# Reordered front of an attention and feed-forward kernel: scores two tiles ahead, fixed VectorE and ScalarE order, two units begun early

## The chip, the cores and the metric

The kernel runs on one core of a Trainium2 chip. The metric is the time of one execution on the device in microseconds (us); the median of 3 runs of the kernel before is 967.41 us (967.27 to 970.9). Names of engines in the trace: PE is TensorE (PEld its weight loads), DVE is VectorE, ACT is ScalarE, POOL is GpSimd, SP is the queue that issues most DMAs.

## The reference: attention, then two feed-forward layers

```python
q_d, k_d, v_d = means of q, k, v over groups of factor=4 positions
out_up    = repeat(softmax(scale * q_d @ k_d.T) @ v_d, 4)     # 144 x 144 per head
scores    = where(abs(pos_i - pos_j) < 4, scale * q @ k.T, -1e9)
out_local = softmax(scores) @ v                               # a band of 7 keys per query
x   = (out_up + out_local) as 2304 tokens x 512
h   = silu(x @ w_gate) * (x @ w_val);  x2  = h @ w_out        # d_ff 1536
h2  = x2 @ w_in;  out = (h2 * clip(h2 + 3, 0, 6) / 6) @ w_out2  # d_ff 2048
```

Four batches, 8 heads, 576 positions, head size 64. The weights arrive as 64-bit numbers and are decoded to 32 bits on the chip.

## The kernel before: a front, then a stream of units

**Blocks and units.** The 2304 tokens are worked in five blocks of 512, 384, 512, 512 and 384 columns. For each block the feed-forward layers run as 68 units, each of 128 rows of a weight: G and V (gate and value), O (out), H and P (second layer). A unit of G, V or H is 12 matmuls into one of two PSUM banks named mm: x and the weights are each split into a high and a low part, and high x high, low x high and high x low are added for four chunks of 128 rows. Attention for batches 1 to 3 runs on VectorE beside the units.

**The front.** Batch 0's attention has no units to hide behind. It is done by `first_batch` on TensorE, 0 to about 64 us of the span. First q and k are turned (`load_T`), with the downsampled attention (`down_scores`, `down_trans`, `down_values`, four chunks of two heads) in between. Then the band is worked in five tiles of 122 queries, the last of 88. For a tile, `scores(i)` makes the masked scores on TensorE, takes the maxima on VectorE (fnm) and the exponentials with their sums on ScalarE (held, eight instructions); `norm(i)` divides on VectorE; `trans(i)` turns the weights on TensorE, ahead of which stand `fill` matmuls on constants (FILL_P of them), and copies the two halves back, one by ScalarE and one by VectorE (turned); `values(i)` multiplies with the values on TensorE, adds the downsampled part, and `put_cols` writes the tile's columns of x (xr), high part by ScalarE, low part by VectorE. PSUM banks are few: tile 0, 2, 4's scores share acc0 and acc1, tile 1, 3's share the mm banks, all turnings share acc2 and acc3, and `down_trans`, `down_values` and `values` share pa and px.

**Weights.** `prefetch(i)` issues five steps for units ahead: load (raw 64-bit, four buffers), `decode_a` on ScalarE (top), `decode_b` on VectorE (w), the copy to `kept`, and `split_unit` (wr, high part on ScalarE, low part on VectorE, for a pair of units). A raw buffer is free for the next load once `decode_b` has read it.

**What sets the order.** Each engine works through its own queue in the order that the program is built with. Instructions under `tc.keep_in_program_order` stand in the order of the code; the others are placed by the scheduler where it expects them to be ready. In the kernel before, the front's matmuls are pinned, VectorE's and ScalarE's work of the front is mostly not, and weight steps are pinned (`behind`) only until `first_batch` ends. `run_unit` splits unit 0 (HALVES = 1) into columns 0 to 244 and 244 to 512, unpinned, so the scheduler put four of its matmuls between those of the last tiles.

Of the kernel before, what the change touches and what calls it, by code (L numbers as in the profile page):

```python
# [32 lines left out]
HALVES = 1  # L33
# [10 lines left out]
FILL_P = (4, 8, 8, 8, 8)  # L44
# [3 lines left out]
def tile_kernel(  # L48
# [85 lines left out]
    front = [True]  # L134

# [134 lines left out]
    def put_cols(bi, col, xv):  # L270

        if bi not in xr:
            xr[bi] = sp.tile([P, NC, 2, UMAX * UT], F32R, tag="xr", name=f"xr{bi}")
        dst = xr[bi][:, :, :, col:col + xv.shape[2]]
        nc.scalar.activation(dst[:, :, 0], xv, AF.Copy)
        nc.vector.tensor_tensor(dst[:, :, 1], xv, dst[:, :, 0].bitcast(F32), op=ALU.subtract)
# [39 lines left out]


    def first_batch():
# [6 lines left out]
        with tc.tile_pool(name="fp", bufs=1) as fp:  # L325
# [125 lines left out]
            for base, sgn in ((-UPAD, -1), (UPAD + 3, 1)):  # L451
                nc.gpsimd.affine_select(
                    out=ups, in_=ups, compare_op=ALU.is_ge, fill=0.0,
                    base=base, pattern=[[-sgn, UPAD + 3 * QT]], channel_multiplier=4 * sgn,
                )
            kT = fp.tile([P, NC, S + 6], F32, name="fkT")
            nc.vector.memset(kT[:, :, :3], 0.0)
            nc.vector.memset(kT[:, :, S + 3:], 0.0)
# [12 lines left out]
            def load_T(w, c):  # L471
                src = qn[w, c // 2]
                for th in range(2):
                    tag = ("acc0", "acc1", "mm", "mm")[turn[0] % 4]
                    turn[0] += 1
                    ps = bank(tag, f"fT{w}{c}{th}", 2 if tag == "mm" else 1)
                    ps = ps[:, :3 * (TT + GJ)].rearrange("p (t n) -> p t n", t=3)
                    for t in range(3):
                        tc.keep_in_program_order(nc.tensor.matmul(
                            ps[:, t], src[:, 3 * th + t, c % 2 * 2:c % 2 * 2 + 2].rearrange("j h d -> j (h d)"),  # L480
                            turner, start=True, stop=True,
                        ))
                    dst = qT[:, c, th * S // 2:(th + 1) * S // 2] if w == "q" else \
                        kT[:, c, 3 + th * S // 2:3 + (th + 1) * S // 2]
                    dst = dst.rearrange("p (t j) -> p t j", t=3)
                    small = (ds if w == "q" else dk)[:, c, th * NJH:(th + 1) * NJH].rearrange("p (t j) -> p t j", t=3)
                    if w == "q":
                        nc.vector.tensor_scalar(dst, ps[:, :, :TT], 0.125, None, op0=ALU.mult)
                        nc.scalar.activation(small, ps[:, :, TT:], AF.Copy, scale=1 / 128)
                    else:  # L490
                        nc.scalar.activation(dst, ps[:, :, :TT], AF.Copy)
                        nc.vector.tensor_copy(small, ps[:, :, TT:])
# [7 lines left out]
            def down_scores(c):  # L500
# [14 lines left out]
                for par in range(2):  # L515
                    nc.vector.tensor_reduce(nm[:, par], pss[par], axis=AX.X, op=ALU.max, negate=True)
                    for half in range(2):
                        nc.scalar.activation(
                            pd[:, par, half], pss[par][:, half], AF.Exp, bias=nm[:, par, half:half + 1],
                        )  # L520
# [4 lines left out]
            def down_trans(c):  # L525
                pd = dst[c]
                for par in range(2):
                    h = 2 * c + par
                    pt = trans_d(lambda qh: pd[:, par, qh], bank(("pa", "px")[par], f"fdT{h}"), together)
                    dpt[h] = fp.tile([NJH, 2, NJ], F32, tag="fdpT", name=f"fdpT{h}", bufs=8)  # L530
                    nc.scalar.activation(dpt[h], pt, AF.Copy)

            def down_values(c):
# [9 lines left out]
                nc.vector.tensor_scalar(sd, po[:, :, :, D:], EPS, 4.0, op0=ALU.add, op1=ALU.mult)  # L543
                nc.vector.reciprocal(sd, sd)
                nc.vector.tensor_tensor(
# [8 lines left out]
            first_max = []  # L554

            def scores(i):
# [27 lines left out]
                for par in range(2):  # L584
                    ps = pss[par][:n, :, :w_]
                    nc.vector.tensor_reduce(nm[:n, :, par], ps, axis=AX.X, op=ALU.max, negate=True)
                    for c in range(NC):
                        nc.scalar.activation(
                            p_[:n, c, par, :w_], ps[:, c], AF.Exp, bias=nm[:n, c, par:par + 1],
                            accum_out=sm[:n, c, par:par + 1],  # L590
                        )
                pe[i], tot[i] = p_, sm
                if i == 0:
                    first_max.append(nm[:n, 0, :1])

            def norm(i):
                n = size(i)
                w_ = n + 6
                nc.vector.tensor_scalar(tot[i][:n], tot[i][:n], EPS, None, op0=ALU.add)
                nc.vector.reciprocal(tot[i][:n], tot[i][:n])  # L600
                nc.vector.tensor_tensor(
# [8 lines left out]
            def trans(i):  # L610
# [3 lines left out]
                for hh in range(2):  # L614
# [9 lines left out]
                    if hh:  # L624
                        nc.vector.tensor_copy(to, ps[:w_, :, :, :n])
                    else:
                        nc.scalar.activation(to, ps[:w_, :, :, :n], AF.Copy)
# [27 lines left out]
            for c in range(NC):  # L655
# [6 lines left out]
                if c == 2:  # L662
                    prefetch(3 - LR)
# [6 lines left out]
            next(ahead)  # L670
            down_values(0)
            down_values(1)
            norm(0)
            trans(0)
            prefetch(4 - LR)
            down_trans(3)
            down_values(2)
            norm(1)
            scores(2)
            down_values(3)  # L680
            prefetch(5 - LR)
            values(0)
            for i in range(1, NT):
                next(ahead, None)
                next(ahead, None)
                trans(i)
                if i + 2 < NT:
                    scores(i + 2)
                if i == 1:
                    prefetch(6 - LR)  # L690
                if i == 2:
                    prefetch(7 - LR)
                if i + 1 < NT:
                    norm(i + 1)
                next(ahead, None)
                values(i)
            for _ in ahead:
                pass
        front[0] = False
# [240 lines left out]
    HIGH, LOW = ((0, 0), (1, 0)), ((0, 1),)  # L940

    def run_unit(i):
# [3 lines left out]
        if kind in "GVH":  # L946
            ps = bank("mm", f"p{kind}{bi}_{f}", 2)[:, :nt]
            x = xr[bi] if kind != "H" else state["x2"]
            cols = [slice(0, nt)]
            if i < HALVES:  # L950
                cols = [slice(0, 244), slice(244, nt)]
            for cs in cols:
                for part in (HIGH, LOW):
                    for c in range(NC):
                        for a, b_ in part:
                            nc.tensor.matmul(  # L956
                                ps[:, cs], r[:, a, c], x[:, c, b_, cs],
                                start=part is HIGH and a == c == 0, stop=part is LOW and c == NC - 1,
                            )
# [93 lines left out]
    for bi in range(NB):  # L1053
# [34 lines left out]
        for i in range(bi * NU, (bi + 1) * NU):  # L1088
            m = i - bi * NU
            prefetch(i)  # L1090
# [66 lines left out]
```

## Time and profile before

| | us |
|---|---|
| median of 3 runs | 967.41 (967.27 to 970.9) |
| profiled execution | 967.38 |
| its span, first to last instruction | 965.7 |
| front: first instruction to the first matmul of unit 2 (pV) | 71.12 |
| mean granted TensorE clock | 0.993 |

A row of the timeline reads: start in us of the span, duration in us, engine, line, operation, output <- inputs, shape, how many in a row, and in brackets the idle time of that engine before it and what ended it. A duration contains the pipeline's latency, so the pace of an engine is taken from the starts of rows that follow each other.

### The profile page before, as it was taken

Reading aid. Unit: us, or ns where it says so; the run is one execution under the profiler, and the core shown is the slowest. Engines: PE = TensorE matmul, PEld = TensorE weight load, DVE = VectorE, ACT = ScalarE, POOL = GpSimd, SP = SyncE. Lnnn points to the kernel's source line nnn. Section 1 sums busy time; section 2 is a strip of 40 time slices with the busy share of each in tenths; the row PEclk is TensorE's granted clock in tenths of the full one; section 3 lists DMA queues with packets and bytes.
Section 4 is the critical chain, followed back from the end, with each engine's and each line's share of the span. In section 5 each row is a group of like instructions: output and inputs, shape, how many; then the busy total and the mean of one; then the engine's idle time right before and its main releaser. Section 6 shows DMA issues by size and latency. Waiting matters only on the chain.

```text
span 965.7 us, 13166 instructions
## 1 busy us (share of the span) xinstructions
PE 948.1 (98%) x4928; PEld 803.2 (83%) x4928; DVE 724.6 (75%) x1059; ACT 501.6 (52%) x928; POOL 110.4 (11%) x125
## 2 busy tenths in 40 slices
PE   9899999999999999999999999999999999999997
PEld 7687888777899988878888778888888788999996
DVE  4678976899979979999774799997337994445652
ACT  4666566876543567553333764443335445444542
POOL 7610002200062300014320000000000000000000
PEclk9999999999999999999999999999999999999999
DMA  8999799866799823359972222462322323443331
GB/s 195 228 270 340 247 366 311 183 198 236 261 246 264 166 86 109 99 188 242 199 157 88 88 67 67 173 216 90 97 100 93 103 88 108 154 131 130 120 122 33
DMA packets 116340, 160.80 MB, mean 167 GB/s; under 512 B 61868, under 2 KB 83756, under 8 KB 116276
## 3 DMA queue, kind: packets, MB, share of 16 engines
q1 hardware_dynamic: 67892, 131.41, 42.7%
q0 software_dynamic: 43488, 10.72, 11.1%
q10 hardware_dynamic: 4896, 17.83, 4.7%
q8 instruction: 39, 0.64, 0.3%
q14 instruction: 25, 0.20, 0.1%
HBM read 137.29 MB, written 22.54 MB: 166 GB/s over the span
## 4 chain that ended last, share of the span: by engine, by line
PE 78%; DVE 7%; DMA 1%; ACT 1%; issue 1%; ACTq 0%; DVEq 0%
PE pH L956 19%; PE aP L998 18%; PE aO L998 13%; PE pV L956 13%; PE pG L956 12%; DVE wr L239 2%; PE pS L881 1%; PE pO L731 1%; DMA w<-in_moe_w_out_dram 1%; DVE xf L856 1%; PE pPT L724 1%; PE px L847 1%; DMA w<-in_moe_w_gate_dram 1%; DVE pv L827 1%; DVE w L225 1%
## 5 line engine op out<-in xcount | busy, mean ns | idle before, releaser
L239 DVE TENSOR_TENSOR wr<-w,wr 128x1024 fp32r<-128x1024 f32 x170 | 207.8, 1222 | 123.8 <-ACT wr L238 123.6
L238 ACT ACTIVATE wr<-w 128x1024 fp32r<-128x1024 f32 x170 | 179.5, 1056 | 119.1 <-issue 57.7
L956 PE MATMUL pH<-x,wr 128*128 128x512 f32 (+1 forms) x960 | 212.2, 372 | 0.0
L998 PE MATMUL aP<-wr,gH 128*128 128x512 f32 x864 | 211.4, 395 | 0.3 <-ACT gH L973 0.3
L956 PEld LDWEIGHTS pH<-x,wr 128*128 128x128 f32 x960 | 173.1, 188 | 25.3 <-issue 2.9
L998 PEld LDWEIGHTS aP<-wr,gH 128*128 128x128 f32 x864 | 159.8, 188 | 34.8 <-issue 2.5
L956 PE MATMUL pG<-xr,wr 128*128 128x512 f32 (+3 forms) x732 | 156.4, 369 | 1.0 <-DVE sl L968 0.6
L956 PE MATMUL pV<-xr,wr 128*128 128x512 f32 (+1 forms) x720 | 153.9, 369 | 0.9 <-ACT sl L962 0.9
L998 PE MATMUL aO<-gV,wr 128*128 128x512 f32 (+1 forms) x720 | 154.4, 371 | 0.0
L956 PEld LDWEIGHTS pG<-xr,wr 128*128 128x128 f32 x732 | 133.3, 191 | 18.5 <-DVE sl L968 1.0
L998 PEld LDWEIGHTS aO<-gV,wr 128*128 128x128 f32 x720 | 132.4, 190 | 16.9 <-DVE gV L974 0.2
L956 PEld LDWEIGHTS pV<-xr,wr 128*128 128x128 f32 x720 | 130.8, 188 | 18.4 <-ACT sl L962 1.8
L971 ACT ACTIVATE h<-pH,consts 128x512 f32<-128x512 f32 (+1 forms) x80 | 51.4, 643 | 59.7 <-PE pH L956 59.5
L973 ACT ACTIVATE gV<-sl 128x512 fp32r<-128x512 f32 (+1 forms) x60 | 35.0, 584 | 85.5 <-DVE sl L968 85.2
L216 ACT ACTIVATE top<-w 128x512 f16<-128x512 bf16 x68 | 52.3, 790 | 22.9 <-DMA w<-in_moe_w_out_dram 7.7
L962 ACT ACTIVATE sl<-pG 128x512 f32<-128x512 f32 (+1 forms) x60 | 33.0, 551 | 59.6 <-PE pG L956 57.0
L973 ACT ACTIVATE gH<-h 128x512 fp32r<-128x512 f32 (+1 forms) x80 | 46.9, 586 | 31.9 <-DVE h L972 31.6
L972 DVE SCALAR_TENSOR_TENSOR h<-h,pH 128x512 f32<-128x512 f32 (+1 forms) x80 | 50.5, 632 | 15.6 <-ACT h L971 15.1
L790 DVE TENSOR_TENSOR pr<-q,k 128x1792 f32<-128x1792 f32 x27 | 54.6, 2021 | 9.4 <-DMA k<-in_k_dram 9.2
L974 DVE TENSOR_TENSOR gH<-h,gH 128x512 fp32r<-128x512 f32 (+1 forms) x80 | 50.6, 633 | 10.9 <-ACT gH L973 10.5
L827 DVE TENSOR_TENSOR pv<-sc,v 128x1792 f32<-128x1792 f32 x27 | 54.6, 2022 | 0.5
L793 DVE TENSOR_REDUCE sc<-pr 128x28 f32<-128x1792 f32 x27 | 54.4, 2015 | 0.1
(131 smaller groups left out, 761.9 us busy)
## 6 DMA issues: line engine op xcount, KB each, us to landing
w<-kept SPq DMA_DIRECT2D x136, 512.0 KB
kept<-w ACTq DMA_DIRECT2D x34, 512.0 KB
w<-in_moe_w_out_dram SPq DMA_DIRECT2D x28, 512.0 KB
w<-in_moe_w_in_dram SPq DMA_DIRECT2D x16, 512.0 KB
w<-in_moe_w_gate_dram SPq DMA_DIRECT2D x12, 512.0 KB
w<-in_moe_w_val_dram SPq DMA_DIRECT2D x12, 512.0 KB
out_dram<-os SPq DMA_DIRECT2D x16, 256.0 KB
dnq<-in_q_dram POOLq DMA_DIRECT2D x24, 144.0 KB, 7.8
```

What stands on the lines that cost most here:

```text
L216: behind(nc.scalar.activation(halves(top[i % 2], 2, F16)[:, :, 1], h3.bitcast(BF16), AF.Copy))
L238: behind(nc.scalar.activation(r[:, :, 0], s, AF.Copy))
L239: behind(nc.vector.tensor_tensor(r[:, :, 1], s, r[:, :, 0].bitcast(F32), op=ALU.subtract))
L790: nc.vector.tensor_tensor(pr, qt[:, a:a + SUB, None, :].to_broadcast([P, SUB, W, D]), win(kt, a, SUB), op=ALU.mult)
L793: nc.vector.tensor_reduce(sc[:, a:a + SUB], pr, axis=AX.X, op=ALU.add)
L827: nc.vector.tensor_tensor(pr, pe[:, a:a + SUB, :, None].to_broadcast([P, SUB, W, D]), win(vt, a, SUB), op=ALU.mult)
L956: nc.tensor.matmul(ps[:, cs], r[:, a, c], x[:, c, b_, cs], start=part is HIGH and a == c == 0, stop=part is LOW and c == NC - 1,)
L971: nc.scalar.activation(h, ps, AF.Relu, scale=1 / 6, bias=half1[:, 0:1])
L972: nc.vector.scalar_tensor_tensor(h, h, 1.0, ps, op0=ALU.min, op1=ALU.mult)
L973: nc.scalar.activation(g[:, 0, :nt], h, AF.Copy)
L974: nc.vector.tensor_tensor(g[:, 1, :nt], h, g[:, 0, :nt].bitcast(F32), op=ALU.subtract)
L998: nc.tensor.matmul(ps, **one, start=f_ == 0 and a == b_ == 0, stop=f_ == nf - 1 and b_ == 1,)
```

## The change

- In `first_batch`, `scores` is cut in two: matmuls and maxima stay, the exponentials become `weights(i)`, placed later in the code.
- In the loop over tiles the order is now `norm(i)`, `scores(i + 2)`, `values(i - 1)`, `trans(i)`, `weights(i + 2)`, then the weight prefetch; it was `trans(i)`, `scores(i + 2)`, prefetch, `norm(i + 1)`, `values(i)`.
- `vec` and `act` (class Ordered) pin every VectorE and ScalarE instruction of the front from `kT` on; `put_cols` is pinned by `behind`. The weight steps stay pinned until unit 3's prefetch (EARLY_W = 4).
- FILL_P goes from (4, 8, 8, 8, 8) to (4, 4, 4, 4, 0).
- HALVES = 2: `begin_unit`, pinned, works 244 columns of unit 0 after `values(2)` and 366 columns of unit 1 after `values(3)`; `run_unit` does columns 244 to 512 and 366 to 512 after the front.

```diff
-FILL_P = (4, 8, 8, 8, 8)
+EARLY_W = 4
+FILL_P = (4, 4, 4, 4, 0)
...
+    def begin_unit(i, n):
+        kind, f, bi = units[i]
+        ps = bank("mm", f"p{kind}{bi}_{f}", 2)
+        products(ps, split[i], xr[bi], slice(0, n), tc.keep_in_program_order)
+        begun[i] = ps, n
...
+            def weights(i):
+                n = size(i)
+                pss, nm = scored.pop(i)
+                for par in range(2):
+                    for c in range(NC):
+                        act.activation(
...
             scores(0)
             ahead = down_sums(1, ["qk"], first_max[0])
+            weights(0)
             down_trans(2)
             down_scores(3)
             scores(1)
+            weights(1)
...
             for i in range(1, NT):
                 next(ahead, None)
                 next(ahead, None)
-                trans(i)
+                norm(i)
                 if i + 2 < NT:
                     scores(i + 2)
                 if i == 1:
-                    prefetch(6 - LR)
+                    down_values(2)
+                    down_values(3)
+                values(i - 1)
+                if i >= NT - HALVES:
+                    begin_unit(i - NT + HALVES, (i - 1) * QT)
+                trans(i)
+                if i + 2 < NT:
+                    weights(i + 2)
+                    prefetch(4 + i - LR)
...
         for i in range(bi * NU, (bi + 1) * NU):
             m = i - bi * NU
+            front[0] = i < EARLY_W
             prefetch(i)
```

ScalarE after the last turning of k, before: fdT is chunk 2 of the downsampled weights turned, fdpT its copy, held tile 0's exponentials, fdpd chunk 3's.

```order
L491 ACTIVATE fkT<-fTk_439 128x288
L531 ACTIVATE fdpT_476<-fdT_471 72x288
L588 ACTIVATE held,fsm_445<-fS_0_447,fnm_446 122x128 x4
L588 ACTIVATE held,fsm_445<-fS_1_448,fnm_446 122x128 x4
L531 ACTIVATE fdpT_483<-fdT_478 72x288
L518 ACTIVATE fdpd_492<-fdS_485,fdnm_491 72x144 x2
```

In the changed kernel the same place of ScalarE's queue reads:

```order
L145 ACTIVATE fkT<-fTk_436 128x288
L145 ACTIVATE held,fsm_442<-fS_0_444,fnm_443 122x128 x4
L145 ACTIVATE held,fsm_442<-fS_1_445,fnm_443 122x128 x4
L145 ACTIVATE fdpT_473<-fdT_468 72x288
L145 ACTIVATE fdpT_480<-fdT_475 72x288
L145 ACTIVATE fdpd_489<-fdS_482,fdnm_488 72x144 x2
```

Both copies of chunk 2 now stand behind tile 0's eight exponentials, where the first stood ahead of them.

ScalarE around the split of units 0 and 1 (wr), before: held and fsm are tile 2's and then tile 3's exponentials and sums, xr and turned belong to tiles 0 and 1.

```order
L588 ACTIVATE held,fsm_612<-fS_0_614,fnm_613 122x128 x4
L588 ACTIVATE held,fsm_612<-fS_1_615,fnm_613 122x128 x4
L216 ACTIVATE top_159<-w_2_265 128x512
L238 ACTIVATE wr_655<-w_0_580 128x2x512
L275 ACTIVATE xr_671<-fO_658 128x4x122
L627 ACTIVATE turned<-fPT_0_678 128x488
L231 DMA kept_125<-w_0_580 128x1024
L588 ACTIVATE held,fsm_698<-fS_0_700,fnm_699 122x128 x4
```

In the changed kernel ScalarE's queue has there:

```order
L288 ACTIVATE xr_686<-fO_673 128x4x122
L145 ACTIVATE turned<-fPT_0_689 128x488
L145 ACTIVATE held,fsm_629<-fS_0_631,fnm_630 122x128 x4
L145 ACTIVATE held,fsm_629<-fS_1_632,fnm_630 122x128 x4
L229 ACTIVATE top_159<-w_2_265 128x512
L251 ACTIVATE wr_717<-w_0_620 128x2x512
```

VectorE in the same place, before (fsm and held in three rows are `norm(2)`):

```order
L225 SCALAR_TENSOR_TENSOR w_0_580<-w_1_257,top_161 128x512
L599 TENSOR_SCALAR fsm_612<-fsm_612 122x8
L600 RECIPROCAL fsm_612<-fsm_612 122x8
L601 TENSOR_TENSOR held<-held,fsm_612 122x1024
L239 TENSOR_TENSOR wr_655<-w_0_580,wr_655 128x2x512
L276 TENSOR_TENSOR xr_671<-fO_658,xr_671 128x4x122
L625 COPY turned<-fPT_1_692 128x488
```

In the changed kernel VectorE's queue has there:

```order
L289 TENSOR_TENSOR xr_686<-fO_673,xr_686 128x4x122
L145 COPY turned<-fPT_1_699 128x488
L238 SCALAR_TENSOR_TENSOR w_0_620<-w_1_257,top_161 128x512
L252 TENSOR_TENSOR wr_717<-w_0_620,wr_717 128x2x512
L145 TENSOR_SCALAR fsm_558<-fsm_558 122x8
L145 RECIPROCAL fsm_558<-fsm_558 122x8
L145 TENSOR_TENSOR held<-held,fsm_558 122x1024
```

The split of units 0 and 1 now stands behind tile 3's exponentials on ScalarE, and ahead of `norm(2)` on VectorE, where it stood behind `norm(2)` and ahead of tile 3's exponentials.

VectorE at the end of the front, before (w are decodings, wr_912 the split of units 2 and 3, wr_954 that of 4 and 5, the last xr rows tile 4's columns):

```order
L276 TENSOR_TENSOR xr_671<-fO_808,xr_671 128x4x122
L625 COPY turned<-fPT_1_841 128x488
L225 SCALAR_TENSOR_TENSOR w_4_910<-w_4_577,top_159 128x512
L239 TENSOR_TENSOR wr_912<-w_2_727,wr_912 128x2x512
L225 SCALAR_TENSOR_TENSOR w_4_910<-w_5_651,top_161 128x512
L276 TENSOR_TENSOR xr_671<-fO_850,xr_671 128x4x122
L625 COPY turned<-fPT_1_879 94x4x88
L225 SCALAR_TENSOR_TENSOR w_6_984<-w_6_724,top_159 128x512
L276 TENSOR_TENSOR xr_671<-fO_885,xr_671 128x4x24
L239 TENSOR_TENSOR wr_954<-w_4_910,wr_954 128x2x512
```

In the changed kernel the end of the front reads on VectorE:

```order
L289 TENSOR_TENSOR xr_686<-fO_851,xr_686 128x4x122
L145 COPY turned<-fPT_1_885 94x4x88
L289 TENSOR_TENSOR xr_686<-fO_891,xr_686 128x4x24
L289 TENSOR_TENSOR xr_906<-fO_891,xr_906 128x4x64
L238 SCALAR_TENSOR_TENSOR w_4_916<-w_4_617,top_159 128x512
L252 TENSOR_TENSOR wr_918<-w_2_789,wr_918 128x2x512
L238 SCALAR_TENSOR_TENSOR w_4_916<-w_5_713,top_161 128x512
L252 TENSOR_TENSOR wr_947<-w_4_916,wr_947 128x2x512
L238 SCALAR_TENSOR_TENSOR w_6_976<-w_6_786,top_159 128x512
```

Three decodings and the split of units 2 and 3 went from ahead of the last tile's columns to behind them.

## Rows read from the trace of the kernel before

**Rows 1.** The page, part 1: busy us (share of the span) and instructions.

```profile
PE 948.1 (98%) x4928; PEld 803.2 (83%) x4928; DVE 724.6 (75%) x1059; ACT 501.6 (52%) x928; POOL 110.4 (11%) x125
```

**Rows 2.** Timeline of PE in the front, 25 to 50 us.

```profile
25.16 1.25 PE L538 MATMUL fdO<-fvd,fdpT 72*72 72x65 f32 x16
...
26.63 1.25 PE L538 MATMUL fdO<-fvd,fdpT 72*72 72x65 f32 x16 [0.22 <-ACT fdpT L531]
...
30.08 0.75 PE L724 MATMUL fdT<-ident,fdpd 72*72 72x72 f32 x8 [0.92 <-DVE tmp L545]
...
33.03 1.57 PE L538 MATMUL fdO<-fvd,fdpT 72*72 72x65 f32 x16 [2.21 <-ACT fdpT L531]
...
41.37 1.05 PE L469 MATMUL fPT<-ident 128*128 128x256 bf16 x8
...
42.26 1.00 PE L620 MATMUL fPT<-ident,held 122*128 122x122 f32 x8
...
43.19 0.64 PE L572 MATMUL fS<-band,pick 64*122 64x512 bf16 x4
...
47.73 1.05 PE L469 MATMUL fPT<-ident 128*128 128x256 bf16 x8
```

**Rows 3.** Windows of 10 us: busy (instructions) by engine, granted clock, DMA share, GB/s.

```profile
30.00:40.00 10.00, 7.71 (x73) 6.39 (x74) 6.78 (x15) 5.12 (x25) 6.86 (x5) 0.83 1.36 226
60.00:70.00 10.00, 10.00 (x70) 8.81 (x69) 6.95 (x10) 6.28 (x10) 0.00 (x0) 0.83 0.92 320
340.00:350.00 10.00, 8.30 (x40) 7.87 (x39) 8.21 (x16) 4.14 (x8) 0.00 (x0) 0.83 0.32 106
```

**Rows 4.** Timeline of PE inside the third of those windows.

```profile
343.66 0.41 PE L847 MATMUL px<-ident,o 128*128 128x128 f32 x2 [1.70 <-DVE o L833]
```

**Rows 5.** Timeline of PE around units 0 to 2.

```profile
67.92 0.64 PE L956 MATMUL pG<-xr,wr 128*128 128x268 f32 x3
...
68.17 0.62 PE L956 MATMUL pG<-xr,wr 128*128 128x512 f32 x2
...
71.12 5.74 PE L956 MATMUL pV<-xr,wr 128*128 128x512 f32 x24
```

**Rows 6.** Timeline of ACT, 26 to 70 us.

```profile
26.16 0.42 ACT L531 ACTIVATE fdpT<-fdT 72x288 f32<-72x288 f32 x1
...
38.07 0.37 ACT L588 ACTIVATE held<-fS,fnm 122x128 f32<-122x128 f32 x1 [4.88 <-DVE fnm L586]
...
40.82 0.81 ACT L216 ACTIVATE top<-w 128x512 f16<-128x512 bf16 x1
...
42.39 0.61 ACT L275 ACTIVATE xr<-fO 128x488 fp32r<-128x488 f32 x1
...
64.23 0.25 ACT L275 ACTIVATE xr<-fO 128x96 fp32r<-128x96 f32 x1 [2.59 <-PE fO L644]
...
68.08 1.28 ACT L962 ACT_TABLE_LOAD   x1 [1.06 <-DVE w L225]
...
69.37 0.60 ACT L962 ACTIVATE sl<-pG 128x512 f32<-128x512 f32 x1
```

**Rows 7.** Timeline of DVE, 37 to 43 us.

```profile
37.34 1.29 DVE L586 TENSOR_REDUCE fnm<-fS 122x4 f32<-122x512 f32 x2 [1.88 <-PE fS L580]
...
38.55 0.15 DVE L543 TENSOR_SCALAR fdsd<-fdO 72x4 f32<-72x4 f32 x1
...
39.28 0.68 DVE L225 SCALAR_TENSOR_TENSOR w<-w,top 128x512 int32<-128x512 int32 x1
...
41.00 0.35 DVE L599 TENSOR_SCALAR fsm<-fsm 122x8 f32<-122x8 f32 x1 [1.04 <-ACT held L588]
...
42.76 1.22 DVE L239 TENSOR_TENSOR wr<-w,wr 128x1024 fp32r<-128x1024 f32 x1
```

**Rows 8.** Timeline of DVE and of PE in the first pass over units.

```profile
107.34 1.23 DVE L239 TENSOR_TENSOR wr<-w,wr 128x1024 fp32r<-128x1024 f32 x1
...
112.08 5.60 PE L956 MATMUL pG<-xr,wr 128*128 128x512 f32 x24
```

More of the change, by code (lines that the diff above doesn't have):

```diff
@@ L32 @@
 WARM = 14
-HALVES = 1
+HALVES = 2
 CLOAD = (0, 4)
@@ L134, in tile_kernel, with __init__, __getattr__, issue @@
     front = [True]
+    class Ordered:
+        def __init__(self, engine):
+            self.engine = engine
+        def __getattr__(self, name):
+            op = getattr(self.engine, name)
+            def issue(*args, **kw):
+                tc.keep_in_program_order(op(*args, **kw))
+            return issue
     def behind(ins):
@@ L315, in down_T, with products @@
             yield
+    HIGH, LOW = ((0, 0), (1, 0)), ((0, 1),)
+    begun = {}
+    def products(ps, r, x, cs, pin=lambda ins: None):
+        for part in (HIGH, LOW):
+            for c in range(NC):
+                for a, b_ in part:
+                    pin(nc.tensor.matmul(
+                        ps[:, cs], r[:, a, c], x[:, c, b_, cs],
+                        start=part is HIGH and a == c == 0, stop=part is LOW and c == NC - 1,
+                    ))
+    def begin_unit(i, n):
[3 more added lines that the diff above has]
+        begun[i] = ps, n
     def first_batch():
@@ L584, in scores @@
                 for par in range(2):
[L585 to L591, printed above, removed]
+                    vec.tensor_reduce(nm[:n, :, par], pss[par][:n, :, :w_], axis=AX.X, op=ALU.max, negate=True)
                 pe[i], tot[i] = p_, sm
+                scored[i] = pss, nm
                 if i == 0:
                     first_max.append(nm[:n, 0, :1])
+            def weights(i):
+                n = size(i)
+                pss, nm = scored.pop(i)
+                for par in range(2):
+                    for c in range(NC):
+                        act.activation(
+                            pe[i][:n, c, par, :n + 6], pss[par][:n, c, :n + 6], AF.Exp,
+                            bias=nm[:n, c, par:par + 1], accum_out=tot[i][:n, c, par:par + 1],
+                        )
             def norm(i):
@@ L668, in first_batch @@
             scores(1)
+            weights(1)
             next(ahead)
             next(ahead)
+            norm(0)
             down_values(0)
             down_values(1)
-            norm(0)
+            scores(2)
             trans(0)
+            down_trans(3)
+            prefetch(3 - LR)
+            weights(2)
             prefetch(4 - LR)
[L676 to L682, printed above, removed]
             for i in range(1, NT):
@@ L689, in first_batch @@
                 if i == 1:
-                    prefetch(6 - LR)
+                    down_values(2)
[7 more added lines that the diff above has]
+                    prefetch(4 + i - LR)
                 if i == 2:
                     prefetch(7 - LR)
-                if i + 1 < NT:
-                    norm(i + 1)
                 next(ahead, None)
-                values(i)
+            values(NT - 1)
             for _ in ahead:
                 pass
-        front[0] = False
         x_done[0] += NG
@@ L946, in run_unit @@
         if kind in "GVH":
-            ps = bank("mm", f"p{kind}{bi}_{f}", 2)[:, :nt]
+            ps, done = begun.pop(i, (None, 0))
+            if ps is None:
+                ps = bank("mm", f"p{kind}{bi}_{f}", 2)
             x = xr[bi] if kind != "H" else state["x2"]
[L949 to L959, printed above, removed]
+            products(ps, r, x, slice(done, nt))
+            ps = ps[:, :nt]
             if kind == "G":
```

42 lines of the change are left out of this document (20 added, 22 removed).

## The prediction, made before the changed kernel ran

> **What bounds the kernel now.** I read the page first: PE is busy for 948.1 of 965.7 us, and no other engine comes near [rows 1]. So what counts is time in which PE stands still, works at the lower clock, or does work that nobody needs. The change touches only the front, so I then read the timeline of PE from 25 us on, where the order of its work first differs, up to the first matmul of unit 2 (pV) at 71.12 [rows 5]. This is the stretch that the sum is made for: 71.12 - 25.16 = 45.96 us [rows 2, 5]. The reader is to see four things in it. PE idles three times: 0.22, 0.92 and 2.21 us, 3.35 together [rows 2]. The granted clock is at its lower level, 1.2 of 2.4 GHz, twice: windows of 10 us with a mean of 0.83 lack 0.17 x 10 = 1.7 us of full speed, and PE had work throughout both stretches, so 3.4 us are lost [rows 3]. Eight fill matmuls take 41.37 to 42.26, 0.89 us or 0.111 each, and there are 4 + 4 x 8 = 36, so 4.0 us [rows 2]. What is left, 45.96 - 3.35 - 3.4 - 4.0 = 35.2 us, is work at full pace.
>
> **The change: work.** 20 fills go: -2.2 us [rows 2]. In the profile they cover no wait, since the weights they stand before were divided long before them. The split of unit 1 costs something: a pass of 12 matmuls has a price per matmul that shrinks with the columns only in part. At the full clock two of 268 columns start 67.92 to 68.17, 0.125 apart, and 24 of 512 take 5.58 us to the next group, 0.233 each, if I count the row's 5.74 less its pipeline end [rows 5]. Between these, 366 columns take 0.165, or 2.0 us for 12. 146 columns lie below the smallest pace that I read at the full clock: 0.068 by columns alone, at most the 0.125 of 268 columns, so 0.8 to 1.5 us; I take 1.2, nearer to the upper end, since the weight load of each matmul does not shrink. Together 3.2 against 2.8 for one pass of 512: +0.4 (0 to +0.7). Unit 0's split is in both kernels.
>
> **The change: waits.** The three idle spells of before go, and five come. I take these in order.
>
> A. ScalarE copies chunk 2's turned weights. Before, the first copy ran ahead of tile 0's exponentials, and PE went from scores(1) straight to `down_values(0)` at 25.16 [rows 2]. Now both copies stand behind the eight exponentials, whose end is where the copy of 26.16 started [rows 6]. That copy frees the bank that `down_values(0)` writes, so PE starts it at 26.16 + 0.42, and waits 1.4 us. Queued behind on PE: `down_values(1)`, scores(2) and all that follows.
>
> B. `values(0)` needs chunk 2's downsampled output from VectorE. From the turning of chunk 3 on, ScalarE copies (0.7, two of the kind at 26.16), decodes (0.7, a row's 0.81 less its end), then VectorE decodes (0.6, row at 39.28), does `norm(1)` (1.7, from 41.00 to 42.76), tile 3's maxima (1.2, from 37.34 to 38.55) and the output (0.7, from 38.55 to 39.28): 5.6 us [rows 6, 7]. PE meanwhile has tile 3's scores (1.4) and two chunks of values (1.1 each, a row's 1.25 less its pipeline end): 3.6 us. It waits 2.0.
>
> C. `trans(2)` needs `norm(2)`, which now stands on VectorE behind the split of units 0 and 1, and that waits for ScalarE's part of the split, behind tile 3's exponentials. From the end of `values(0)`: four fills 0.44, half of tile 1's turning 0.47, its copy 0.5, the exponentials 38.07 to 40.82 (2.75), decoding and split 40.82 to 42.39 (1.57), VectorE's split 1.22, `norm(2)` 1.7, and some 0.2 for handing over: 8.85 us [rows 2, 6, 7]. PE has to do in that time what before stood between 41.37 and 47.73, 6.36 us, with four fills fewer (-0.44), four fills of its own (+0.44), and the scores of the short last tile in place of tile 3's (0 to -0.35): 6.0 to 6.36 [rows 2]. It waits 2.5 to 2.8; I take 2.7.
>
> D. The rest of units 0 and 1 needs tile 4's columns at once, where before the part of unit 0 below column 244 lay in between. ScalarE's copy takes 0.25, with the handing over 0.45 [rows 6].
>
> E. pV needs unit 0's bank, freed by the first Silu. On ScalarE this stands behind tile 4's two copies (0.4), a decoding (0.65), a split (0.95) and the table load (1.28), and takes 0.6: 3.9 us from the last value matmul [rows 6]. PE has D, 1.5, 1.2 and 0.2 us of small turnings, 3.35. It waits 0.6.
>
> The waits of before go, since ScalarE's copies are now ahead of PE there: -3.35. New ones: 1.4 + 2.0 + 2.7 + 0.45 + 0.6 = 7.2.
>
> **The change: the clock.** Without any stretch at the lower clock the sum is 35.2 + 0.4 + 1.8 (16 fills) + 7.2 = 44.6 us against 45.96: -1.35. How often the clock falls is the open term. Before, it stayed up behind an idle spell of 0.92, fell behind 2.21 in the front and behind 1.70 in the middle of the kernel [rows 2 to 4], and fell once more near 64 us, where PE had not idled at all, only worked through the last tile's small matmuls [rows 3]. Spells B and C are above 1.70, so I expect a fall behind each; A lies between 0.92 and 1.70 and is open; at the end of the front 12 matmuls of 366 columns now stand before the last tile's small ones, but its fills are gone: open too. So two falls, with 0 and 4 as bounds. One costs 1.7 us while PE has work, less where part of it lies in the spell that brought it: I take 1.5. Two: +3.0.
>
> The sum is -1.35 + 3.0 = +1.65 us. It is made against the profiled execution, 967.38 us, which is the median of the runs (967.41) to 0.03, so about 969.0. Behind pV I add nothing: the same units follow, and the decodings that come later there are the third rival.
>
> **The rivals.** *The clock holds, or falls once.* Then A to E are paid and the rest gained: 967.4 - 1.35 = 966.0 with no fall, 967.5 with one. For it: the single matmul passes of 244 and 366 columns and the short distance between scores. Against it: spells of 2.0 and 2.7 beside the row of 1.70. The Trainium skill (TensorE: Matmul & The Clock Gate, section Why this matters for your kernels) lays falls to idle gaps between bursts longer than any that I count here; by that rule the time would be 966.0 too, but the fall near 64 us, with PE busy for 10.00 of 10 us [rows 3], does not agree with it.
>
> *It does what it says.* Scores two tiles ahead are meant to give VectorE and ScalarE time before a tile's turning. If B and C come out near nothing, because the chain in C starts earlier than `trans(1)` on PE, the sum is -1.35 - 4.7 = -6.05, or 961.3, with no fall, since those two spells bring the falls. Against it: the queues are fixed, and the rows printed for the change put `norm(2)` behind the split.
>
> *Slower: the first pass runs out of weights.* Three decodings of 0.6 and a split of 1.2 (3.0 us of VectorE, and as many on ScalarE) moved behind the last tile, and the loads that wait for those decodings' buffers start later. The split that the first pass needs soonest after its making ends at 107.34 + 1.23 = 108.57, and PE uses it at 112.08 [rows 8]. From the point where the delay exceeds these 3.5 us PE waits for every microsecond more. With four falls (+6.0) and 2 us of such waiting: 967.4 - 1.35 + 6.0 + 2 = 974.
>
> **How the numbers follow.** Two or three falls with the waits as summed (969.0 to 970.5): 0.45. The clock holds or falls once: 0.25. Slower by late weights and four falls: 0.18. It does what it says: 0.10. Something else within 0.5%: 0.02. Half a per cent of 967.4 is 4.8 us, about what a measurement of this kernel can tell from no change: faster means under 962.6, slower over 972.2. Only the case that does what it says lies below, only the late weights above: 0.10, 0.72, 0.18. The predicted time is that of the likeliest case, 969.0. The range goes from 963.5, a little under the clock that holds with spell C half as long, to 974, the slower rival's time, and leaves out the case of 961.3 and the far end of late weights.
>
> **What would show it.** In the changed kernel's timeline: `down_values(0)` starts near 26.6 behind ScalarE's copy (A); `values(0)` waits for VectorE (B); `trans(2)` waits for about 2.7 us with `norm(2)` late, and VectorE idle ahead of the split of units 0 and 1 (C); pV starts between 70 and 73.5 where it was 71.12. If `trans(2)` does not wait, the prediction's main term is wrong. If windows of the front show the lower clock never, or three times and more, the clock's term is. If PE waits for the splits (wr) between 75 and 115 us, the third rival is at work.

## The result: 0.9% slower, with the lower clock in the front for 17 us

The changed kernel takes 976.05 us (median of 5 runs, 972.64 to 979.68) beside 967.27 for the kernel before (5 runs, 964.24 to 970.9): a ratio of 1.0089 (95% interval 1.0061 to 1.0118). The prediction said 969.0, at most 974.0: the time lies above its range.

The profiled execution took 976.03 us. Part 1 of its page is the counterpart of [rows 1]: PE has 8 matmuls fewer (20 fills go, 12 come with unit 1's split) and is still busy for 1.4 us more.

```profile
PE 949.5 (97%) x4920; PEld 803.7 (82%) x4920; DVE 723.6 (74%) x1059; ACT 502.7 (52%) x928; POOL 110.3 (11%) x125
```

PE's timeline of the front, after, is the counterpart of [rows 2, 5]. The columns are start, duration, engine, line, operation, output <- inputs, shape, count, and in brackets the idle time before the row with what ended it.

```profile
26.23 2.26 PE L570 MATMUL fdO<-fvd,fdpT 72*72 72x65 f32 x32 [1.49 <-ACT fdpT L145]
37.62 0.45 PE L676 MATMUL fO<-tmp 72*128 72x122 f32 x2 [2.13 <-DVE fdsd L145]
...
51.19 1.05 PE L658 MATMUL fPT<-ident,held 122*128 122x122 f32 x8 [1.26 <-DVE held L145]
...
58.05 2.92 PE L338 MATMUL pG<-xr,wr 128*128 128x244 f32 x12
...
72.33 3.04 PE L338 MATMUL pG<-xr,wr 128*128 128x268 f32 x24 [0.35 <-ACT xr L288]
...
76.59 0.72 PE L338 MATMUL pV<-xr,wr 128*128 128x512 f32 x2 [0.96 <-ACT sl L993]
```

All five waits A to E are there, each ended by the instruction that the prediction named. The first matmul of unit 2 (pV) starts at 76.59 where it started at 71.12 [rows 5]: 5.47 of the 8.65 us between the two profiles are lost in the front. The other 3.18 are lost behind it.

The windows of the same execution show what became of the clock (window, its length, busy time and count by engine, PEclk, DMA share, GB/s), the counterpart of [rows 3].

```profile
30.00:39.50 9.50, 7.37 (x86) 6.28 (x84) 6.91 (x15) 5.54 (x23) 8.05 (x7) 1.00 1.37 234
39.60:46.30 6.70, 6.70 (x44) 5.03 (x44) 1.93 (x3) 3.51 (x17) 4.91 (x5) 0.50 1.15 96
46.50:53.00 6.50, 5.24 (x45) 3.55 (x44) 4.60 (x8) 3.51 (x11) 2.48 (x2) 1.00 1.24 170
53.30:63.30 10.00, 10.00 (x49) 8.15 (x48) 3.36 (x6) 4.12 (x15) 0.00 (x0) 0.50 0.59 197
...
340.00:350.00 10.00, 9.34 (x60) 8.96 (x59) 9.81 (x15) 4.78 (x10) 0.00 (x0) 1.00 0.30 107
```

Two falls, as predicted, and each begins some 2 us behind one of the two waits for a VectorE result. But they are long. The clock stays at its lower level (0.50, so 1.2 of 2.4 GHz) through the whole of 39.6 to 46.3 and of 53.3 to 63.3, and PE has work for all of both. The group of 12 matmuls of 244 columns at 58.05 takes 2.92 us there. With the two ends, 39.56 to 46.39 and 53.21 to 63.45, it is 17.1 us at half pace, so 8.5 lost, where [rows 3] lacked 1.7 + 1.7 in the same part of the kernel. The fall that [rows 3] has near 344 us does not come after the change.

Behind pV, PE waits longer at three places. These rows are again from its timeline.

```profile
194.29 0.71 PE L771 MATMUL pO<-pT,dnv 72*64 72x144 f32 x6 [1.51 <-DMA dnv<-in_v_dram]
262.24 0.41 PE L887 MATMUL px<-ident,o 128*128 128x128 f32 x2 [2.10 <-DVE o L873]
322.01 2.32 PE L338 MATMUL pG<-xr,wr 128*128 128x384 f32 x12 [1.51 <-DVE sc L841]
...
353.75 0.41 PE L887 MATMUL px<-ident,o 128*128 128x128 f32 x2 [1.71 <-DVE o L873]
```

The last is the wait of [rows 4], 1.70 there, unchanged. The other three are new or longer; the second was 0.42 at its place before (236.57 us).

### The profile page after: what moved, and what is told of

It reads as the page before. It is cut to its first block, busy times and chain, and to the rows that moved or that the text cites. A ratio compares the mean times of both kernels' runs of the same rounds, so it can differ in the third digit from the quotient of the medians.

```text
span 974.2 us, 13153 instructions
## 1 busy us (share of the span) xinstructions
PE 949.5 (97%) x4920; PEld 803.7 (82%) x4920; DVE 723.6 (74%) x1059; ACT 502.7 (52%) x928; POOL 110.3 (11%) x125
## 4 chain that ended last, share of the span: by engine, by line
PE 68%; DVE 13%; DMA 10%; issue 5%; ACT 3%; POOL 0%; SPq 0%; DVEq 0%; ACTq 0%; POOLq 0%
PE pH L338 15%; PE aP L1029 15%; PE pG L338 10%; PE aO L1029 10%; PE pV L338 10%; DMA k<-in_k_dram 3%; DVE wr L252 3%; DVE w L238 2%; DMA dnv<-in_v_dram 2%; DMA w<-in_moe_w_out_dram 1%; DVE pv L867 1%; DVE pr L830 1%; DVE xf L896 1%; PE fO L676 1%; DMA w<-in_moe_w_in_dram 1%
## 5 line engine op out<-in xcount | busy, mean ns | idle before, releaser
L338 PE MATMUL pG<-xr,wr 128*128 128x512 f32 (+5 forms) x744 | 156.7, 365 | 3.3 <-DVE sc L841 1.5
L238 DVE SCALAR_TENSOR_TENSOR w<-w,top 128x512 int32<-128x512 int32 x68 | 45.7, 684 | 11.8 <-ACT top L229 9.5
```

Source lines behind the costliest of these rows:

```text
L238: behind(nc.vector.scalar_tensor_tensor(w32[i // 2][:, i % 2].bitcast(I32), h12, 13, top[i % 2], op0=ALU.logical_shift_right, op1=ALU.bitw ...
L338: pin(nc.tensor.matmul(ps[:, cs], r[:, a, c], x[:, c, b_, cs], start=part is HIGH and a == c == 0, stop=part is LOW and c == NC - 1,))
```

## Experiments

For each kernel the runs give a span and a mean granted clock. Their product, span x (1 - clock), is how much full-speed time the clock held back, idle or not; the table gives its mean over the runs of the kernel, and the rest of the span. The end of the program, where PE runs out of work, is in it for all kernels alike. "Before" is the kernel before on the same chip in the same session. It had between 967.27 and 969.06 us in these sessions, so medians of different rows compare to some 1 to 2 us; the ratios are free of that. A profile is one execution: those of e1, e3 and e7 (972.19, 959.12 and 960.12 us) lie 3.7 to 4.9 us below the medians of their kernels, that of e5 (976.13) 2.1 above.

| kernel | median us (runs) | before | ratio, 95% interval | held back by the clock | rest of span |
|---|---|---|---|---|---|
| changed | 976.05 (5) | 967.27 | 1.0089 (1.0061 to 1.0118) | 11.7 | 962.6 |
| e1_fills_back | 977.09 (6) | 969.06 | 1.0081 (1.0049 to 1.0113) | 10.6 | 964.0 |
| e2_norm_first | 970.21 (12) | 969.06 | 1.0018 (0.9996 to 1.0040) | 10.3 | 958.6 |
| e3_no_waits | 963.10 (12) | 969.06 | 0.9957 (0.9930 to 0.9985) | 5.0 | 957.0 |
| e4_no_waits_fills | 968.12 (12) | 969.06 | 0.9991 (0.9969 to 1.0012) | 5.4 | 960.5 |
| e5_waits_covered | 974.04 (12) | 968.99 | 1.0057 (1.0028 to 1.0085) | 4.7 | 967.7 |
| e6_b_gone | 963.76 (12) | 968.99 | 0.9954 (0.9929 to 0.9979) | 3.7 | 958.8 |
| e7_no_fills | 963.82 (12) | 968.99 | 0.9966 (0.9941 to 0.9990) | 6.4 | 956.4 |
| e8_early0 | 970.48 (12) | 968.99 | 1.0028 (1.0002 to 1.0054) | 10.7 | 958.1 |
| e9_covered_again | 970.34 (12) | 968.18 | 1.0028 (0.9995 to 1.0062) | 4.9 | 964.2 |
| e10_b_alone | 973.07 (12) | 968.18 | 1.0046 (1.0018 to 1.0073) | 11.0 | 960.2 |
| before (35) | 968.99 | | | 7.6 | 959.0 |

So of the changed kernel's 7.7 us over the kernel before (the last two columns added, 974.3 against 966.6), the clock holds 4.1 and the rest 3.6. This split is rough: what the clock held back in the five runs of the changed kernel goes from 7.8 to 16.6 us. The theory that the runs test is that standing still in the front (A, B, C) brings the long falls; its rivals are that the missing fills do, or that the waits cost their own length and the clock falls from the front's small matmuls anyway.

### e1: are the missing fills the cause?

```diff
-FILL_P = (4, 4, 4, 4, 0)
+FILL_P = (4, 8, 8, 8, 8)
```

> The changed kernel with the old fills (4, 8, 8, 8, 8) back; VectorE's and ScalarE's order stays word for word, TensorE has 20 small matmuls more (2.2 us). Theory 'fills': the missing fills let the clock fall for long (17.1 us at the lower level in the changed kernel's front, 6.8 before); with them back at most 7 us of it remain, so 5 us come back and 2.2 are paid: about 973.2 where the changed kernel takes 976.05. Theory 'waits': the idle spells bring the falls, fills change nothing: 976.05 + 2.2 = 978.3, and the front still has 17 us at the lower clock. For the 3.2 us that were lost behind the first matmul of unit 2 both theories expect no change.

977.09 us, no better than the changed kernel, with 10.6 us held back by the clock instead of 11.7. The theory that the 20 fills held the clock up where they stood falls by the time (it named 973.2, the other 978.3): they come back and the loss stays. They stand ahead of the turnings, behind the waits A and B. The profile, 4.9 us under the median, is between the two theories: the long fall behind wait B is there, but behind a wait of 1.36 us at C (51.51 us) none comes. Its windows:

```profile
30.00:40.00 10.00, 8.12 (x89) 6.59 (x87) 6.24 (x15) 5.34 (x21) 7.53 (x6) 0.93 1.35 217
40.00:50.00 10.00, 10.00 (x74) 7.16 (x73) 3.25 (x6) 6.09 (x21) 8.40 (x6) 0.72 1.07 106
50.00:60.00 10.00, 8.61 (x74) 7.06 (x74) 7.17 (x13) 5.41 (x21) 0.00 (x0) 1.00 1.01 234
```

### e2 and e3: take the waits away

e2 puts `norm(2)` on VectorE ahead of the split of units 0 and 1, and `norm(3)` ahead of the decodings that follow; 8 rows of VectorE's order change, none of PE's.

```diff
                 if i + 2 < NT:
                     weights(i + 2)
-                    prefetch(4 + i - LR)
-                if i == 2:
-                    prefetch(7 - LR)
...
                 norm(i)
+                if i == 2:
+                    prefetch(5 - LR)
+                if i == 3:
+                    prefetch(6 - LR)
+                    prefetch(7 - LR)
                 if i + 2 < NT:
                     scores(i + 2)
```

> The changed kernel with one thing undone: norm(2) stands ahead of the split of units 0 and 1 on VectorE again (and norm(3) ahead of the decodings of units 2 and 3); eight rows of VectorE's queue change place, every other queue is the same. The wait of trans(2) for norm(2), 1.26 us in the changed kernel (1.8 with what its fills covered), should go. Theory 'waits': with it goes the fall of the clock behind it (10.2 us at the lower level, 5.1 lost): 970 to 971. Theory 'fills': only the wait goes, the front keeps 14 us or more at the lower clock: 974.5. If the time stays at 976, the wait was not on the path.

e3 also puts `down_trans(2)` ahead of tile 0's exponentials (A) and `down_values(2)` and `(3)` ahead of tile 3's scores (B).

```diff
+            down_trans(2)
             weights(0)
-            down_trans(2)
...
+            down_values(2)
+            down_values(3)
             for i in range(1, NT):
...
-                if i == 1:
-                    down_values(2)
-                    down_values(3)
                 values(i - 1)
```

> The changed kernel with all three waits taken away by order alone: chunk 2's copies ahead of tile 0's exponentials, down_values 2 and 3 ahead of tile 3's scores, norm(2) ahead of the split. Their 1.49 + 2.13 + 1.26 = 4.9 us go. Theory 'waits': the clock falls at most once, 5 us more come back: about 966, better than the kernel before (967.3). Theory 'fills': the clock falls as long as in the changed kernel: 971.

e2 gives 970.21 and e3 963.10: 5.8 and 12.9 us less than the changed kernel, for waits of 1.26 and of 4.9 us in its profile. e3 is faster than the kernel before too, by 0.4%. The windows of e3's front, from an execution of 959.12 us, show why it is more than the waits (columns as above):

```profile
30.00:40.00 10.00, 9.51 (x113) 7.62 (x110) 7.38 (x19) 6.98 (x29) 7.21 (x6) 1.00 1.33 224
40.00:50.00 10.00, 10.00 (x83) 7.69 (x84) 7.78 (x12) 8.79 (x35) 6.78 (x5) 1.00 1.12 162
50.00:60.00 10.00, 9.56 (x79) 7.42 (x76) 3.73 (x7) 2.11 (x5) 2.74 (x2) 1.00 1.17 220
60.00:70.00 10.00, 9.98 (x52) 9.06 (x53) 6.24 (x9) 8.18 (x12) 0.00 (x0) 0.83 0.69 212
```

PE is busy for 39.05 of these 40 us and the clock is down once only, in the last ten, the stretch that was down in [rows 3] as well. In e2, which keeps A and B, the window behind B is at the lower level from end to end:

```profile
38.50:48.50 10.00, 10.00 (x57) 7.07 (x58) 3.20 (x7) 3.51 (x17) 8.77 (x7) 0.50 1.24 114
```

So e2's 970.21 is the time that the theory 'waits' named (970 to 971), but by luck: the gain is hardly in the clock (10.3 us against 11.7), it is in the rest, 4.0 us for a wait of 1.26. ScalarE's and VectorE's later work stands behind the same place, and e2's profile has neither the 0.96 us ahead of pV (E) nor the 1.51 ahead of pG.

### e4 and e7: what are fills worth where nothing waits?

e4 is e3 with 20 fills more, FILL_P = (4, 8, 8, 8, 8); e7 is e3 with none, FILL_P = (0, 0, 0, 0, 0).

> The kernel without the three waits, and with the old fills (4, 8, 8, 8, 8). Theory 'waits': 966 + 2.2 = 968. Theory 'fills': 976.05 - 4.9 - 5.1 + 2.2 = 968.2 as well, but then it is faster than the one without waits and with few fills (971), where 'waits' has it slower by 2.2.

> e3 without any fill (the 16 that are left in front of the tiles' turnings go). Theory 'idle': they are matmuls nobody needs, the clock stays up as long as no wait of over 1 us comes: 963.1 - 16 x 0.111 = 961.3, and only a little less where they covered the wait for a tile's division. Rival 'fills hold the clock': the falls come back in the front, one or two of 3.41 us or more, 963 to 966.

968.12 with 36 fills, 963.10 with 16, 963.82 with none. More of them cost (3.5 us in the rest, of which 2.2 are the fills); the last 16 make no difference that these runs can tell: 0.6 us less in the rest, 1.4 more held back by the clock. For e7 the theory 'idle' had 961.3, too low by 2.5, and the time lies in the rival's range (963 to 966). Its profile does not bear the rival out: the front has one short fall, as e3's has, and another fall comes at 247 us behind a px that waited 1.94. So fills ahead of the turnings do little or nothing for the clock. e4's profile had a wait of 3.12 us for a load (dnv) at 186 us as well, which moves about from kernel to kernel.

### e6 and e10: wait B, with C gone and with C there

e6 is e2 with B's edit, e10 is the changed kernel with B's edit alone.

```diff
+            down_values(2)
+            down_values(3)
             for i in range(1, NT):
...
-                if i == 1:
-                    down_values(2)
-                    down_values(3)
                 values(i - 1)
```

> The kernel of e2 (norm first, no wait C) with down_values(2) and (3) ahead of tile 3's scores, so that wait B (1.9 us) goes too and A (1.5) stays. Theory 'idle': the wait goes, and with it the fall behind it, which was in e2's profile 10.24 us long from 38.3 us: 970.2 - 1.9 - 1.7 to 5.1 = 963.2 to 966.6. Rival 'only the wait': 970.2 - 1.9 = 968.3, the fall near 38 us still there. Rival 'A is the one that counts' (e3's gain lies in A alone): 970.

> The changed kernel with wait B alone taken away (down_values(2) and (3) ahead of tile 3's scores; 16 rows of TensorE's and 10 of VectorE's order), A and the late norm(2) of C stay. Theory 'each wait has its own fall': 976.05 - 2.1 for the wait - 3.4 for the fall of 39.56 = 970.5. Rival 'C takes it over' (the end of C is set by ScalarE's and VectorE's queues, so TensorE comes earlier and waits longer there): the wait ahead of trans(2) grows from 1.26 to 3 or more, a fall still follows, 973.5 to 975.5.

With C gone, taking B away gives 6.4 us, all of it from the clock (10.3 to 3.7 held back; the rest is 0.2 more). Wait A is still there in e6, 1.51 us, and in this profile a short fall follows it (28 to 31.5 us):

```profile
20.00:30.00 10.00, 8.49 (x108) 7.58 (x108) 6.76 (x17) 8.23 (x42) 7.60 (x11) 0.91 1.06 269
30.00:40.00 10.00, 9.66 (x101) 7.69 (x100) 6.77 (x15) 5.34 (x21) 7.83 (x7) 0.92 1.37 222
```

With C there, taking B away gives 3.0 us and the clock holds back as much as ever (11.0). The timeline of e10 shows PE coming earlier to `trans(2)` and standing there longer, and the window behind it lies at the lower level for 12 us:

```profile
47.94 1.89 PE L658 MATMUL fPT<-ident,held 122*128 122x122 f32 x8 [2.82 <-DVE held L145]
```

```profile
48.00:60.00 12.00, 12.00 (x56) 9.64 (x57) 5.50 (x10) 4.99 (x20) 2.74 (x2) 0.50 1.14 217
```

So B and C are one loss in two places: what the clock holds back stays over 10 us when either goes (10.3, 11.0) and is 3.7 when both go. The theory that each wait has a fall of its own does not hold; the rival, that C takes over what B leaves, describes this profile, though its time (973.5 to 975.5) and its wait (3 or more) were a little high.

### e5 and e9: leave the lateness, cover the standing still

Both keep the changed kernel's order of VectorE, ScalarE and the queues, and put fill matmuls that nobody needs where PE stood still. In e5 the first fills stood in a bank (acc2) that is itself free only later; e9 mends that.

```diff
             norm(0)
+            fill(bank("acc0", "coverA"), 12)      # e5: acc2, 14
             down_values(0)
...
+                if i == 1:
+                    fill(bank("acc2", "coverB"), 20)
                 values(i - 1)
...
-FILL_P = (4, 4, 4, 4, 0)
+FILL_P = (4, 4, 28, 4, 0)                          # e5: (4, 4, 16, 4, 0)
```

> The changed kernel with fill matmuls put exactly where TensorE stood still: 14 ahead of down_values(0) (wait of 1.49 us), 20 ahead of values(0) (2.13), 12 more ahead of trans(2) (1.26), at 0.111 us each 5.1 us for 4.9 us of waiting. No other engine's order differs, and nothing comes any earlier. Theory 'idle' (standing still brings the lower clock, which lasts 17 us there): the three waits are now work, the falls of 39.56 and 53.21 us do not come, 976.05 + 0.2 - 8.5 = 967.8, and 969.5 if one short fall stays. Rival 'late' (the length of the waits and what they delay is the loss, the clock falls from the small matmuls of the front whatever stands between them): 976.3, with 10 us or more at the lower clock before 72 us.

> The changed kernel with fills where TensorE stood still, placed so that they do not wait themselves as e5's did: 12 ahead of down_values(0) in the bank that tile 0's first exponentials free (e5's first fills stood in a bank that was free only 1.0 us after the wait they were to cover, and began at 27.08 after 2.25 us idle), 20 ahead of values(0), 24 more ahead of trans(2). No other engine's order differs. Theory 'idle': waits A, B, C under 0.5 us each, no fall in the front or one short one; share of the clock lost per run 4 to 6 us of the span against 11.7 in the changed kernel; pV at 70 to 73; behind pV as in the changed kernel 899.4 us, so 969.5 to 972.5. Rival 'late' (clock falls with the small matmuls whatever stands between them): 976 to 978, 10 us or more lost to the clock.

e9's timeline of PE:

```profile
24.68 1.48 PE L501 MATMUL coverA<-ident 128*128 128x256 bf16 x12
26.25 2.26 PE L570 MATMUL fdO<-fvd,fdpT 72*72 72x65 f32 x32
...
35.35 2.35 PE L501 MATMUL coverB<-ident 128*128 128x256 bf16 x20
37.54 0.38 PE L676 MATMUL fO<-tmp 72*128 72x122 f32 x2
...
46.09 3.23 PE L501 MATMUL fPT<-ident 128*128 128x256 bf16 x28
49.43 1.05 PE L658 MATMUL fPT<-ident,held 122*128 122x122 f32 x8
```

`down_values(0)` and `values(0)` begin where they began in the changed kernel, 26.25 against 26.23 and 37.54 against 37.62: nothing comes earlier up to there. From there on the work runs at full pace up to 66.9 us, where one short fall comes, and pV starts at 70.88 instead of 76.59, at a place where e9 has issued 56 matmuls more. The time is 970.34, 5.7 us less than the changed kernel, with 4.9 us held back by the clock instead of 11.7. The windows of e9's front:

```profile
30.00:40.00 10.00, 10.00 (x112) 8.58 (x111) 6.73 (x15) 5.60 (x23) 8.26 (x6) 1.00 1.30 226
40.00:50.00 10.00, 9.89 (x95) 7.61 (x95) 5.30 (x9) 5.98 (x21) 6.58 (x6) 1.00 1.15 155
50.00:60.00 10.00, 9.97 (x83) 7.55 (x83) 6.68 (x13) 5.41 (x21) 1.92 (x2) 1.00 1.17 233
60.00:70.00 10.00, 9.56 (x68) 8.46 (x67) 3.95 (x7) 4.74 (x8) 0.00 (x0) 0.84 0.12 31
```

The rival 'late' (976 to 978) falls. This is the experiment that shows the cause: the same lateness, with matmuls in place of the standing still, has no long falls.

e5 gives the same for the clock (4.7 us) and not for the time, which is neither theory's (967.8 to 969.5, or 976.3). Two of its spells stayed, here from PE's timeline, so its 46 fills came on top of them: 5.1 us at 0.111 each, and the rest is 5.1 us longer.

```profile
27.08 1.69 PE L501 MATMUL coverA<-ident 128*128 128x256 bf16 x14 [2.25 <-ACT fdpd L145]
51.75 1.05 PE L658 MATMUL fPT<-ident,held 122*128 122x122 f32 x8 [1.41 <-DVE held L145]
```

It says something about the theory as well. A spell of 2.25 us, as long as the one of [rows 2] that brought a fall, brought none here, and the windows from 30 to 40 and from 40 to 50 us have PE busy for 10.00 of 10 and the clock at 1.00. It is not the length of one spell that decides. Nor do e5 and e9 tell apart whether the fills hold the clock by ending the standing still or by adding work on either side of it: in e5 two of three spells stay, and the long falls are gone as well.

### e8: is the wait for o behind the front due to the pinned weight steps?

e8 is e3 with `front[0] = False` in place of `front[0] = i < EARLY_W`, so that the weight steps of the first units are pinned only in the front's loop.

> e3 with the weight steps of the first units pinned only until the front's loop ends, as before the change (EARLY_W without effect). 156 places of VectorE's and 148 of ScalarE's order change behind the front. All five kernels with the change's order waited 1.87 to 2.10 us for o ahead of the second px (249 to 262 us), the kernel before 0.42 at 236.57. Theory 'pinned': with the pin gone that wait falls to 0.4, 963.1 - 1.5 = 961.6, and the waits of px sum to 3.0 as before. Rival 'not from the pin' (it comes from the front's own order, through which VectorE and the loads stand otherwise): the wait stays near 1.9, 963.1. Rival 'the pin was needed': PE waits for splits (wr) in the first 40 us behind the front, over 964.5.

Both what the first theory and what the last rival name happen, the latter at a place that none of them named. The wait for o falls from about 1.9 to 0.64 us, and px waits for 3.2 us in all, 3.0 before the change. But a decoding that is now free to move lands on ScalarE ahead of tile 3's copy (turned), waits 5.14 us for its load, and PE stands 6.86 us behind it in the front. PE's timeline at both places, then ScalarE's:

```profile
58.51 0.68 PE L682 MATMUL fO<-turned,vw 128*64 128x122 f32 x4 [6.86 <-ACT turned L145]
...
240.36 0.41 PE L888 MATMUL px<-ident,o 128*128 128x128 f32 x2 [0.64 <-DVE o L874]
```

```profile
57.26 0.78 ACT L229 ACTIVATE top<-w 128x512 f16<-128x512 bf16 x1 [5.14 <-DMA w<-in_moe_w_val_dram]
...
57.91 0.54 ACT L145 ACTIVATE turned<-fPT 128x488 f32<-128x488 f32 x1
```

970.48 us, 7.4 over e3, 5.7 of it held back by the clock. The pin pays for itself in the front and costs some 1.3 us at 250.

## Why the prediction was wrong, step by step

| term | predicted | in the profile after |
|---|---|---|
| A, `down_values(0)` behind ScalarE's copies | 1.4 | 1.49 |
| B, `values(0)` behind VectorE | 2.0 | 2.13 |
| C, `trans(2)` behind `norm(2)` | 2.7 | 1.26 |
| D, tile 4's columns | 0.45 | 0.35 |
| E, pV behind the first Silu | 0.6 | 0.96 |
| the five waits | 7.2 | 6.19 |
| lost to the clock in the front | 3.0 | 8.5 |
| fills and the split of unit 1 | -1.8 | about -2.5 |
| front, against before | +1.65 | +5.47 |
| behind pV | 0 | +3.18 |

**The work** came out 0.7 us below what was costed: what is left of 5.47 when the waits (6.19 - 3.35) and the clock (8.5 - 3.4) are taken off is -2.5. Some 0.4 of that lies ahead of the stretch that the sum covers, since PE is through with scores(1) at 24.74 (26.23 - 1.49) where it was at 25.16.

**The waits** were right in kind, place and nearly in sum. C's chain ran as it was written down: the turned half copied at 43.37, exponentials to 46.58 (2.74 us, estimated 2.75), decoding and split on ScalarE, and then VectorE, from its timeline:

```profile
48.33 1.23 DVE L252 TENSOR_TENSOR wr<-w,wr 128x1024 fp32r<-128x1024 f32 x1 [2.88 <-ACT wr L251]
49.48 0.16 DVE L145 TENSOR_SCALAR fsm<-fsm 122x8 f32<-122x8 f32 x1
49.67 0.20 DVE L145 RECIPROCAL fsm<-fsm 122x8 f32<-122x8 f32 x1
49.91 1.23 DVE L145 TENSOR_TENSOR held<-held,fsm 122x1024 f32<-122x1024 f32 x1
51.05 0.99 DVE L145 TENSOR_REDUCE fnm<-fS 88x4 f32<-88x376 f32 x2
```

PE waited only 1.26 because it came late itself, at half pace since 39.56. In e10, with B gone, it comes at full pace and waits 2.82. The prediction added C's wait and B's fall as though neither knew of the other.

**The clock** is the step that failed: "One costs 1.7 us while PE has work ... I take 1.5. Two: +3.0". The count of two was right and their places were right. The price was read from windows of [rows 3] that all happened to hold a short stretch, and was used as the price of any. Here the two cost 3.4 and 5.1 us. The bounds went wrong in the same way: four falls at 1.5 are 6.0, less than these two. What sets the length was not measured by itself. But the long stretches in the front (in the profiles of the changed kernel, e1, e2, e8 and e10) all have a wait of over 1 us right ahead (in e8 and e10 the fall begins within it), and mostly the front's small matmuls in them; e3, e6, e7 and e9, in which B and C are gone or covered, have falls of 3.4 us (one each, two in e6), e4 and e5 none in the front. With 8.5 in place of 3.0 and the waits as they came, the prediction's own sum gives 967.4 - 1.35 - 1.0 + 8.5 = 973.5. This is just inside its range, so it takes the next step as well to come out above it.

The Trainium skill (TensorE: Matmul & The Clock Gate, section A second HAM failure mode: psum-queue depth-cycling) describes a second way beside the long gap: in one of its kernels brief idling between groups of matmuls came often enough to make the clock swing between its two levels, which cost throughput. The traces agree with that one as far as they go: spells of 1.49, 2.13 and 1.26 us within 27 us, and two falls. The prediction was right to set the gap rule of the same page aside, and did not look at this one.

**"Behind pV I add nothing"** was the second step that failed, by 3.2 us in the profile and by part of the 3.6 in the means. Three places make it up: 1.68 more ahead of one px, 1.51 ahead of pO and 1.51 ahead of pG, less the 1.7 of the fall near 344 us that did not come. The first is in all kernels of this order with the pins (1.87 to 2.94) and gone without them (e8, 0.64): it goes with EARLY_W. On VectorE, the changed kernel has a decoding there that waits for its buffer, with o's last addition queued behind it:

```profile
259.94 0.69 DVE L238 SCALAR_TENSOR_TENSOR w<-w,top 128x512 int32<-128x512 int32 x1 [2.17 <-DMA kept<-w]
260.55 1.22 DVE L252 TENSOR_TENSOR wr<-w,wr 128x1024 fp32r<-128x1024 f32 x1
261.68 0.42 DVE L873 TENSOR_TENSOR o<-pv 128x256 f32<-128x256 f32 x1
```

The wait ahead of pG is in the changed kernel, e5 and e9 (0.68 to 1.51) and in no other; the wait of pO for a load is between 0 and 3.1 us in kernels that differ little. What sets these two is open.

**The rivals.** "Slower: late weights" named this sign and 974 with the wrong place: PE does not wait for a split between 75 and 115 us. Its four falls are nearest to the truth in size. "It does what it says" (961.3, chance 0.10) is what e3, e6 and e7 give, 963.1 to 963.8: the look-ahead works once three steps are ahead of what they stood behind.

## What to carry to other kernels

When waits and small matmuls come close together, don't price a fall of the clock by a stretch seen elsewhere; as an upper bound take the whole stage at half pace. Here taking away 4.9 us of waits gave 12.9. When an engine's order is written by hand, look behind each instruction of another stage (a split, a decoding) for what it now holds up, and take the order from the consumer that waits first: moving `norm(2)` ahead of the split (and `norm(3)` ahead of the decodings) was worth 5.8 us. If a wait on TensorE can't be removed, matmuls on constants placed in it, not beside it, gave back 5.7 us.

## What the runs showed of the hardware

The lower level of the clock lasted anything from 3.4 us (e3's last window, a mean of 0.83 over 10 us) to over 12 (e10's) at a time. What brings it is not one idle spell's length: in e9 PE stood 2.94 us ahead of a px at 256 us and the clock stayed up, in e5 it stood 2.80 us ahead of a pO at 192 us and the clock fell. Their windows, e9's and then e5's:

```profile
250.00:260.00 10.00, 7.05 (x33) 5.55 (x32) 6.30 (x13) 4.22 (x7) 0.00 (x0) 1.00 0.77 297
```

```profile
190.00:200.00 10.00, 7.69 (x35) 6.03 (x36) 6.59 (x9) 4.42 (x10) 0.00 (x0) 0.83 0.49 153
```

The busy time is, if anything, lower where the clock stayed. Wait A tells the same: at 1.49 to 1.51 us a fall followed it in the profiles of e2 and e6, and none in those of the changed kernel, e1 and e10. Runs of one kernel differ by the clock too: e3's fastest took 959.08 us at a mean clock of 0.998, its slowest 969.59 at 0.992, which by span x (1 - clock) is some 6 of the 10.5 us between them. With twelve runs of each kernel the intervals of the table reach 2 to 3 us to either side.
